# Exchanging the chunk parities of every second head in an RWKV-6 kernel, so that two bursts of quarter-array products stand side by side

## The chip, the cores and the metric

The kernel runs on one core of one Trainium2 chip. The metric is the device time of one execution in microseconds; the kernel before takes 603.1 us (median of 3 runs, 601.58 to 604.65). The profiled execution spans 601.8 us with a mean granted TensorE clock of 0.997.

## The reference, cut to what matters

The first half is a linear attention with a decaying state (RWKV-6, 4 batches, 8 heads, 768 steps, head size 48), the second a feed-forward block with an exact GELU:

```python
state = zeros((B, H, D, D))
for t in range(S):
    cur = einsum('bhd,bhe->bhde', u[None] * kt, vt)
    y[:, :, t] = einsum('bhd,bhde->bhe', rt, state + cur)
    state = wt[:, :, :, None] * state + einsum('bhd,bhe->bhde', kt, vt)
...
h = x @ w_in                    # 3072 x 384 by 384 x 2048
g = 0.5 * h * (1.0 + erf(h / sqrt(2)))
out = g @ w_out                 # by 2048 x 384
```

Everything is fp32.

## The kernel before, in words

**Segments.** The 4 x 768 steps are cut into 8 segments of T = 384 steps (`x` = 0 to 7); two follow each other in one batch, so every odd segment starts from the states of the segment before it. A segment has NC = 6 chunks of C = 64 steps. The 8 heads are taken as 4 pairs; in a pair, head g = 0 lies on partitions 0 to 63 and head g = 1 on partitions 64 to 127 (`half[g]`). Two pairs make a part b, so that index i (NI = 6) runs over the pairs of a part and the couples of chunks, and p is the parity of a chunk inside its couple.

**Attention of a segment**, `attention(x, unit)`, is a generator whose `yield`s cut it into slots:

1. Products of r and k within a chunk give the matrix of a chunk, built up by levels (`halves` for segments 0 and 1, `quarters` from segment 2 on). Each product is 64x64x64: contraction over `half[g]`, output on `half[p]` (`d[half[p], g, ...]`, L468 and L596). So four of them use the four quarters of the TensorE array at once. The results are copied into `a_sb` (`at`): parity p on `half[p]`, head g in the free dimension.
2. k is transposed, so that time lies on partitions: in segments 0 and 1 by whole TensorE transposes of 128x128 (L680), later by VectorE's transposes of 32x32 blocks, twelve small DMAs that move blocks (L542) and four copies on ScalarE (L690).
3. `kv` (L706): k transposed times v for each chunk, contraction over `half[p]`. VectorE's `chain_states` (L721, L726) makes from it the state at each chunk's start, one `scalar_tensor_tensor` for each chunk and pair of heads.
4. `y` = `inside` + the products with the states, summed in PSUM. `inside` (L747) multiplies v by the chunk's matrix: contraction over `half[p]`, output on `half[g ^ swap(b)]` of bank `p`. The products with the states (L791) contract over `half[g]` and write the same places. Where p differs from g, two products that add to one place come from different rows of the array. The `fences` between them are small VectorE copies that read the last element of each bank of `y` (L757, L759): they have to wait for `inside`, and the products with the states have to wait for them.
5. `y` goes to `xT`, the input of the feed-forward block: copies on ScalarE (L814, L817) and, for the fourth pair, six DMAs (L821).

PSUM holds `y` of one part as one tile of two banks (`pair`), a bank for each parity; only the first part of segment 0 (`split`) has two tiles of one bank. The tiles come from the same pool as `kv`, so `y` follows `kv` in its banks.

**The feed-forward block**, `mlp(x)`, runs on 128x128 weights: products h (L925, L1051), GELU on ScalarE, products with `w_out` (L1065, L1197), with sums of quarters (L917 to L921, L893) that save one product in eight. Results leave PSUM by ScalarE or VectorE (such as L1119, L1162, L1188).

**Order.** The scheduler is manual: each engine runs its instructions in the order of the program. That order is written out in `PLAN`: for each segment x a string whose letters take the next slot of a stream: "." `mlp(x - 1)`, "s" the attention of x, "f" the first slots of the attention of x + 1, "l" loads, "w" masks and sums of weights, "c" conversion of weights, "x" the sums of xT. Segment 0 isn't in `PLAN`; it runs before, with filler products (`keep_warm`) and the loads beside it.

In a slot for `y`, the lines that the change touches are these:

```python
inside()
fences()
yield
for i in range(NI):
    for p in range(2):
        for b in range(np_):
```

Of the kernel before, what the change touches and what calls it, by code (L numbers as in the profile page):

```python
# [10 lines left out]
F32 = mybir.dt.float32  # L11
# [9 lines left out]
C = 64  # L21
# [15 lines left out]
HALFWAY = 2  # L37
PLAN = {
    1: (
        "ccsc.cs...c.c.csccc.cs.sccc.l.csccccssc.cccs.c..cccs.sc.ccslcsc.scsclc.c.scssl.clc.wcsc.cc"  # L40
        "wsc.l.cs.cclcc.cc.wlwlcc.c.cwcs...wwfs..w...wfwl...s.w..f..wfw...wffffffffw"
    ),
    2: (
        ".......s.l.wsslw.swssss.s.s.sss.lssls.ssssssw..s.swl..w..ww.s.w.s.sslls.ll.slf.wfs..f.xxx."
        ".xx"
    ),
    3: (
        "ss.l....ss.ss...ls.sl.....s..s....sss.s..ss.ssss.ssl...ssls..ssss..ss...s.s..ls..sl..sslls"
        "f.s..fsf.fl.f.xx..xfxx"
    ),  # L50
    4: (
        "...s.s..ss...sl.s..s..l.ssl.ss.ssss.s.s.ss...sss..sssls.s.sls...s.s.l...slsls...sl.sf.fs.f"
        "xxx.lx...x"
    ),
    5: (
        "s.sl....s.s...slss...s.s.l...s....ssls.sls..s.ssssl.ss...ss.s.ss.sss..s.s.....s.ssls.s.l.l"
        "sf.s.ffs.ff..xx..xfxxl"
    ),
    6: (
        ".s..slss.......s.s.s...sll.ssls.sssssl..s.ss...sss..sssss....ssl..ss....slsss...lsl.sf...f"  # L60
        "xxl.xf..xx"
    ),
    7: (
        "s.s.s.s....s..ss.s...s...s.....ss.ss.s.ss.sss.ss...sss..ss.sssss.......s.s..sss.s..s.s...x"
        "xx..xx"
    ),
}

# [6 lines left out]
def kernel(  # L75
# [215 lines left out]
    def make_fine():  # L291
        nc.vector.tensor_tensor(out=fine_mask, in0=s_qs[FINE], in1=t_block, op=ALU.is_equal)
        nc.vector.tensor_tensor(out=later, in0=t_all, in1=s_qs[1], op=ALU.is_ge)
        nc.vector.tensor_tensor(out=fine_mask, in0=fine_mask, in1=later, op=ALU.bitwise_and)

        nc.gpsimd.memset(places, 0.0)
        for z in range(4):
            o = slice(z * 32, (z + 1) * 32)
            v = places[o]
            v = bass.AP(tensor=v.tensor, offset=v.offset, ap=[v.ap[0], [128 + 1, FINE], [FINE, 32]])  # L300
            nc.gpsimd.tensor_copy(out=v, in_=ident[o, o].unsqueeze(1).to_broadcast([32, FINE, 32]))

    def make_quarter_masks():
        make_fine()
# [64 lines left out]
    def attention(x, unit):  # L369
# [91 lines left out]
        def products(bs, right, width):  # L461
            d = pair("d")
            n = 0
            for b in bs:
                for i in range(NI):
                    for g in range(2):
                        for p in range(2):
                            nc.tensor.matmul(d[half[p], g, n * width:(n + 1) * width],  # L468
                                             lhsT=kc[half[g], b, i, p], rhs=right(half[g], b, i, p),
                                             start=True, stop=True)  # L470
                    n += 1
            return d[:, :, 0:n * width]
# [62 lines left out]
        kt_q = k.rearrange("p (g n d) -> p g n d", g=2, d=G)  # L535
        moves = [(src, dst) for dst in range(4) for src in range(4) if src != dst]

        def block_of_kt(dst, src):
            return kt_q[dst * 32:(dst + 1) * 32, src // 2, :, src % 2 * 32:src % 2 * 32 + 32]

        def move_block(dma, src, dst):
            dma.dma_start(out=block_of_kt(dst, src), in_=kb[src * 32:(src + 1) * 32, dst])  # L542

        def blocks_of_k():
            k32 = k.rearrange("p (n a j) -> p n a j", a=4, j=32)
# [5 lines left out]
        def quarters():  # L551
# [28 lines left out]
            for h in QUARTERS:  # L580
                m, r4, t4, s0, s1, s2 = views(h)

                def burst(first, behind):

                    d = pair("d")
                    if behind == n_b and h == FINE:
                        for a in range(FINE):
                            for g in range(2):
                                nc.tensor.matmul(fine_of(d, g)[:, a * n_b:], lhsT=places[half[g], a],  # L589
                                                 rhs=fine_sb[half[g], 0:FINE - a, a],  # L590
                                                 start=(a == 0), stop=True, skip_group_check=True)
                    for n in range(first, behind):
                        i = n - first
                        for g in range(2):
                            for p in range(2):
                                nc.tensor.matmul(d[half[p], g, i * 3 * C // 2:(i + 1) * 3 * C // 2],  # L596
                                                 lhsT=kc[half[g], n // NI, n % NI, p],
                                                 rhs=rx[half[g], 2 * n + p], start=True, stop=True)
                    return d
# [74 lines left out]
        if x < 2:  # L674
            kts = []
            for b in range(np_):
                kt_ps = pair("kt_ps")
                for i in range(NI):
                    o = (i % N3) * 128
                    nc.tensor.transpose(kt_ps[:, i // N3, o:o + 128], k[:, (b * NI + i) * 128:(b * NI + i + 1) * 128], ident)  # L680
                kt = kx[:, parts[b] * Q * T:(parts[b] + 1) * Q * T].rearrange("p (i g d) -> p i g d", g=2, d=G)
                nc.scalar.copy(out=kt.rearrange("p (b i) g d -> p b (i g d)", b=2), in_=kt_ps[:, :, 0:N3 * 128])
                kts.append(kt)

            def k_t(b, i, p, g):
                return kts[b][half[p], i, g, :]
        else:

            for z in range(4):
                nc.scalar.copy(out=block_of_kt(z, z), in_=kb[z * 32:(z + 1) * 32, z])  # L690

            def k_t(b, i, p, g):
                return kt_q[half[p], g, b * NI + i]
        yield

        def vs(b, i, g):
# [4 lines left out]
        for b in range(np_):  # L701
            kv_ps = pair("kv_ps")
            for i in range(NI):
                for p in range(2):
                    for g in range(2):
                        nc.tensor.matmul(kv_ps[half[g], p, i * D:(i + 1) * D], lhsT=k_t(b, i, p, g),  # L706
                                         rhs=vs(b, i, g)[half[p], 0:D], start=True, stop=True)
            kvs.append(kv_ps[:, :, 0:NI * D].rearrange("p c (q i e) -> p q i c e", q=Q, e=D))
        yield

# [22 lines left out]
        split = x == 0 and parts[0] == 0  # L733
        ys = []

        def inside():

            for b in range(np_):
                if split:
                    y = [ps.tile([128, BANK], F32, name="y_ps", tag="mm", bufs=2) for _ in range(2)]  # L740
                else:
                    y_ps = pair("y_ps")
                    y = [y_ps[:, c] for c in range(2)]
                for i in range(NI):
                    for p in range(2):
                        for g in range(2):
                            nc.tensor.matmul(y[p][half[g ^ swap(b)], i * C:(i + 1) * C], lhsT=vs(b, i, g)[half[p]],  # L747
                                             rhs=at[half[p], g, b * NI + i, :], start=(i == 0), stop=True, skip_group_check=True)
                ys.append((y, None if split else y_ps))

        def fences():

            for y, y_ps in ys:
                fence = wk.tile([128, 2], F32, name="fence")
                if split:
                    for c in range(2):
                        nc.vector.tensor_copy(out=fence[:, c:c + 1], in_=y[c][:, NI * C - 1:NI * C])  # L757
                else:
                    nc.vector.tensor_copy(out=fence, in_=y_ps[:, :, NI * C - 1])  # L759

        if x == 0:

            inside()
            yield
            for z in last_r:
                z()
            yield
            chain_states(range(NC - 1 + int(first)))
            fences()
            yield  # L770
        else:
            for c in range(0, NC, 2):
# [1 line left out]
                if x > 1 and c + 2 < NC:  # L774
                    yield
            yield
            inside()
            fences()
            yield

        for i in range(NI):
            for p in range(2):
                for b in range(np_):
                    q, c3 = divmod(i, N3)
                    for g in range(2):
                        c = 2 * c3 + (p + g) % 2
                        src, c0 = (st, c - 1) if c else (before, NC - 1)
                        if src is None:
                            continue
                        o = ((parts[b] * Q + q) * NC + c0) * D  # L790
                        nc.tensor.matmul(ys[b][0][c % 2][half[g ^ swap(b)], i * C:(i + 1) * C],  # L791
                                         lhsT=src[half[g], o:o + G], rhs=rc[half[g], b, i, c % 2],
                                         start=False, stop=True, skip_group_check=True)
        if split:
            for c, copy in enumerate((nc.scalar.copy, nc.vector.tensor_copy)):
                for z in range(2):
# [544 lines left out]
```

## Time and profile before

| engine | busy us | share of the span | instructions |
|---|---|---|---|
| TensorE, matmuls | 587.2 | 98% | 7442 |
| TensorE, weight loads | 514.3 | 85% | 7442 |
| VectorE | 459.9 | 76% | 878 |
| ScalarE | 261.3 | 43% | 604 |
| GpSimd | 8.4 | 1% | 24 |

| group | instructions | busy us | mean ns |
|---|---|---|---|
| `inside`, L747, matmul 64x64x64 | 768 | 13.8 | 222 |
| with the states, L791, matmul 64x64x64 | 704 | 14.4 | 225 |
| `kv`, L706, matmul | 768 | 14.6 | 220 and 227 |
| transposes of k, L680 | 24 | 3.1 | 274 |
| `fences`, L759 and L757, VectorE copy | 15 and 2 | 2.2 and 0.3 | 161 and 154 |
| states, L721, VectorE | 160 | 29.0 | 258 |

One fp32 product of the code is two matmul instructions in the trace (a transpose is one). The busy time of a group is the time in which at least one of its instructions runs; quarter-array products overlap four at a time, so 96 of them, 218 ns each, last only about 1.5 us.

By time, the segments' `y` bursts end near 43, 120, 185, 258, 322, 396, 459 and 533 us; from there to 601.8 us only the last feed-forward block remains. The first 44 us are segment 0, which is short of work for TensorE; after it, TensorE is busy nearly without a break.

### The profile page before, as it was taken

Reading aid. Unit: us, or ns where it says so; the run is one execution under the profiler, and the core shown is the slowest. Engines: PE = TensorE matmul, PEld = TensorE weight load, DVE = VectorE, ACT = ScalarE, POOL = GpSimd, SP = SyncE. Lnnn points to the kernel's source line nnn. Section 1 sums busy time; section 2 is a strip of 40 time slices with the busy share of each in tenths; the row PEclk is TensorE's granted clock in tenths of the full one; section 3 lists DMA queues with packets and bytes.
Section 4 is the critical chain, followed back from the end, with each engine's and each line's share of the span. In section 5 each row is a group of like instructions: output and inputs, shape, how many; then the busy total and the mean of one; then the engine's idle time right before and its main releaser. Section 6 shows DMA issues by size and latency. Waiting matters only on the chain.

```text
span 601.8 us, 17215 instructions
## 1 busy us (share of the span) xinstructions
PE 587.2 (98%) x7442; PEld 514.3 (85%) x7442; DVE 459.9 (76%) x878; ACT 261.3 (43%) x604; POOL 8.4 (1%) x24
## 2 busy tenths in 40 slices
PE   8879999999999999999999999999999999999997
PEld 4566666656699999999999999899999999989997
DVE  8979999998878977798857968798857979631211
ACT  2346656033433545245742554235652456225510
POOL 3100000000000000000000000000000000000000
PEclk9989999999999999999999999999999999999999
DMA  5739564120053101440052210413033100300000
GB/s 199 221 115 365 178 211 125 67 76 19 3 128 116 37 21 17 122 123 19 2 120 83 64 53 5 117 47 113 2 60 94 43 1 1 68 28 6 0 14 26
DMA packets 50571, 46.79 MB, mean 78 GB/s; under 512 B 31680, under 2 KB 35904, under 8 KB 50496
## 3 DMA queue, kind: packets, MB, share of 16 engines
q1 hardware_dynamic: 50400, 45.62, 25.0%
q8 instruction: 58, 0.95, 0.7%
q14 instruction: 17, 0.14, 0.1%
q10 hardware_dynamic: 96, 0.07, 0.1%
HBM read 36.24 MB, written 4.72 MB: 68 GB/s over the span
## 4 chain that ended last, share of the span: by engine, by line
PE 91%; DVE 2%; SPq 2%; issue 2%; DMA 1%; ACT 0%; DVEq 0%; ACTq 0%
PE o_ps L1065 27%; PE h_ps L925 16%; PE u_ps L925 13%; PE h_ps L1051 11%; PE o_ps L1197 5%; PE d L596 5%; PE d L468 3%; PE y_ps L791 2%; PE kv_ps L706 2%; PE y_ps L747 2%; PE u_ps L1065 2%; PE warm L240 2%; SPq L542 1%; SPq L821 1%; PE d L589 1%
## 5 line engine op out<-in xcount | busy, mean ns | idle before, releaser
L925 PE MATMUL h_ps<-xT,w_in_sb 128*128 128x192 f32 x480 | 96.3, 331 | 1.4 <-DVE o_sb L1162 0.8
L925 PEld LDWEIGHTS h_ps<-xT,w_in_sb 128*128 128x128 f32 x480 | 79.6, 190 | 5.3 <-DVE o_sb L1162 1.5
L1051 PE MATMUL h_ps<-xT,w_in_sb 128*128 128x384 f32 x192 | 64.5, 491 | 0.0
L1051 PEld LDWEIGHTS h_ps<-xT,w_in_sb 128*128 128x128 f32 x192 | 35.7, 190 | 23.6
L612 ACT COPY a_sb<-d 32x320 f32<-32x320 f32 (+5 forms) x108 | 39.2, 363 | 3.5 <-PE d L596 1.7
L1065 PE MATMUL o_ps<-w_out_sb,g 128*128 128x192 f32 x224 | 40.0, 327 | 0.0
L1065 PEld LDWEIGHTS o_ps<-w_out_sb,g 128*128 128x128 f32 x224 | 36.8, 190 | 0.6
L925 PE MATMUL u_ps<-s,w_in_sb 128*128 128x192 f32 x192 | 35.1, 326 | 0.0
L1197 PE MATMUL o_ps<-w_out_sb,g 128*128 128x384 f32 x96 | 32.9, 493 | 0.0
L925 PEld LDWEIGHTS u_ps<-s,w_in_sb 128*128 128x128 f32 x192 | 31.9, 190 | 0.0
L1054 ACT ACTIVATE g<-h_ps 128x384 f32<-128x384 f32 (+1 forms) x32 | 14.0, 436 | 40.3 <-PE h_ps L1051 40.3
L817 ACT COPY ysb<-y_ps 128x384 f32<-128x384 f32 x8 | 3.8, 480 | 60.9 <-PE y_ps L791 48.5
L1125 DVE TENSOR_TENSOR u<-o_ps,p 128x192 f32<-128x192 f32 x7 | 2.5, 358 | 36.0 <-PE o_ps L1065 36.0
L596 PE MATMUL d<-kx,rkw 64*64 64x96 f32 x1152 | 29.9, 247 | 0.0
L596 PEld LDWEIGHTS d<-kx,rkw 64*64 64x64 f32 x1152 | 24.9, 133 | 5.7 <-issue 3.2
L721 DVE SCALAR_TENSOR_TENSOR st<-st,tot_sb,kv_ps 128x48 f32<-128x48 f32 x160 | 29.0, 258 | 0.6 <-PE kv_ps L706 0.4
L979 DVE TENSOR_TENSOR g<-g,o_sb 128x384 f32<-128x384 f32 x24 | 13.2, 549 | 21.2 <-ACT o_sb L961 21.2
L1065 PE MATMUL o_ps<-w_out_sb,f 128*128 128x192 f32 x160 | 29.1, 331 | 0.0
L1065 PE MATMUL o_ps<-w_out_sb,e 128*128 128x192 f32 x160 | 28.5, 329 | 0.0
L1065 PE MATMUL o_ps<-t,g 128*128 128x192 f32 x160 | 28.4, 330 | 0.0
L468 PEld LDWEIGHTS d<-rkw 64*64 64x64 f32 x1152 | 18.7, 134 | 10.9 <-issue 3.9
L1065 PE MATMUL o_ps<-t,s 128*128 128x192 f32 x160 | 27.9, 327 | 0.0
(164 smaller groups left out, 1213.2 us busy)
## 6 DMA issues: line engine op xcount, KB each, us to landing
rkw<-in_rkw_dram SPq DMA_DIRECT2D x54, 256.0 KB, 3.5
raw<-in_w_out_dram SPq DMA_DIRECT2D x8, 768.0 KB, 4.5
v_in<-in_v_dram SPq DMA_DIRECT2D x8, 584.0 KB, 4.1
raw<-in_w_in_dram SPq DMA_DIRECT2D x5, 768.0 KB, 7.8
out_dram<-o_sb SPq DMA_DIRECT2D x20, 192.0 KB, 2.1
rkw<-kx SPq DMA_DIRECT2D x72, 48.0 KB, 2.1
raw<-in_w_in_dram SPq DMA_DIRECT2D x9, 256.0 KB, 3.4
rkw<-in_rkw_dram SPq DMA_DIRECT2D x8, 288.0 KB, 3.5
```

The source lines that it names most:

```text
L240: nc.tensor.matmul(t, lhsT=zeros[:, 0:128], rhs=zeros, start=True, stop=True)
L468: nc.tensor.matmul(d[half[p], g, n * width:(n + 1) * width], lhsT=kc[half[g], b, i, p], rhs=right(half[g], b, i, p), start=True, stop=True)
L596: nc.tensor.matmul(d[half[p], g, i * 3 * C // 2:(i + 1) * 3 * C // 2], lhsT=kc[half[g], n // NI, n % NI, p], rhs=rx[half[g], 2 * n + p], s ...
L612: nc.scalar.copy(out=at[z, :, first:behind, (a + 1) * h:], in_=d[z, :, :, o:o + (3 - a) * h])
L706: nc.tensor.matmul(kv_ps[half[g], p, i * D:(i + 1) * D], lhsT=k_t(b, i, p, g), rhs=vs(b, i, g)[half[p], 0:D], start=True, stop=True)
L721: nc.vector.scalar_tensor_tensor(out=stq[:, q, c], in0=stq[:, q, c - 1] if c else b4[:, q, NC - 1], scalar=totq[:, q, c:c + 1], in1=kvs[q ...
L925: nc.tensor.matmul(o, lhsT=lhsT, rhs=rhs, start=start, stop=True, skip_group_check=True)
L979: nc.vector.tensor_add(g_of(q, 0, 1), g_of(q, 0, 1), z)
L1051: nc.tensor.matmul(h_ps, lhsT=w_in_sb[:, f // FI, j, f % FI * 128:(f % FI + 1) * 128], rhs=xT[:, j, :], start=(j == 0), stop=(j == NJ - 1))
L1054: nc.scalar.activation(out=gs[group][:, f % FG, 0:t], in_=h_ps[:, 0:t], func=AF.Gelu)
L1065: nc.tensor.matmul(o, lhsT=lhs(j), rhs=rhs(j), start=start and j == 0, stop=(j == HF - 1), skip_group_check=True)
L1197: nc.tensor.matmul(o, lhsT=block(i, f // HF, f % HF), rhs=w_out_sb[:, f, :], start=(f == 0), stop=(f == NF - 1))
```

## The change

It exchanges, for head g = 1 of every pair, the two parities: the chunk of parity p now lies on `half[p ^ g]`. The matrices (`d`, `a_sb`), v (laid out so on the host), k transposed and the identity blocks in `places` follow. Then `inside` for the even chunks contracts over the same rows as the products with the states for the even chunks, and only the odd chunks come from other rows. The order becomes: `inside(1)`, the fence, `inside(0)`, the states for even chunks, the states for odd chunks. It is for having nothing of the other work between `inside` and the products with the states, so that both make one burst, with the fence's time covered by the even chunks. The fence reads only the odd chunks' bank, and moves from VectorE to ScalarE.

Two things follow. In segments 0 and 1 k is no longer transposed by whole transposes but by 64x64 products with the identity, four to a couple of chunks, since each quarter has to land elsewhere. And the slots of `y` are fewer by one from segment 2 on, so the whole `PLAN` is another one; slots of all streams stand in another order, the bursts of L596 and `kv` too.

```diff
-                            nc.tensor.matmul(d[half[p], g, n * width:(n + 1) * width],
+                            nc.tensor.matmul(d[half[p ^ g], g, n * width:(n + 1) * width],
...
-            v = bass.AP(tensor=v.tensor, offset=v.offset, ap=[v.ap[0], [128 + 1, FINE], [FINE, 32]])
-            nc.gpsimd.tensor_copy(out=v, in_=ident[o, o].unsqueeze(1).to_broadcast([32, FINE, 32]))
+            for part in range(2):
+                to = bass.AP(tensor=v.tensor, offset=v.offset + part * C, ap=[v.ap[0], [128 + 1, FINE], [FINE, 16]])
+                a = o.start + 16 * (part ^ z // 2)
+                nc.gpsimd.tensor_copy(out=to, in_=ident[o, a:a + 16].unsqueeze(1).to_broadcast([32, FINE, 16]))
...
-                    o = (i % N3) * 128
-                    nc.tensor.transpose(kt_ps[:, i // N3, o:o + 128], k[:, (b * NI + i) * 128:(b * NI + i + 1) * 128], ident)
+                    for p in range(2):
+                        for g in range(2):
+                            nc.tensor.matmul(kt_ps[half[p ^ g], g, i * G:(i + 1) * G], lhsT=kc[half[g], b, i, p],
+                                                rhs=ident[half[g], half[g]], start=True, stop=True)
...
+        def inside(c):
+            for i in range(NI):
+                for b in range(np_):
+                    for g in range(2):
+                        nc.tensor.matmul(ys[b][0][c][half[g ^ swap(b)], i * C:(i + 1) * C], lhsT=vs(b, i, g)[half[c ^ g]],
+                                         rhs=at[half[c ^ g], g, b * NI + i, :], start=(i == 0), stop=True, skip_group_check=True)
+
+        def before_chunks(par):
+            for i in range(NI):
+                for b in range(np_):
...
+                        nc.tensor.matmul(ys[b][0][par][half[g ^ swap(b)], i * C:(i + 1) * C],
+                                         lhsT=src[half[g], o:o + G], rhs=rc[half[g], b, i, par],
+                                         start=False, stop=True, skip_group_check=True)
 
         def fences():
 
-            for y, y_ps in ys:
-                fence = wk.tile([128, 2], F32, name="fence")
-                if split:
-                    for c in range(2):
-                        nc.vector.tensor_copy(out=fence[:, c:c + 1], in_=y[c][:, NI * C - 1:NI * C])
-                else:
-                    nc.vector.tensor_copy(out=fence, in_=y_ps[:, :, NI * C - 1])
+            for y, _ in ys:
+                fence = wk.tile([128, 1], F32, name="fence")
+                nc.scalar.copy(out=fence, in_=y[1][:, NI * C - 1:NI * C])
...
             yield
-            inside()
+            places_of_y()
+            inside(1)
             fences()
-            yield
-
-        for i in range(NI):
-            for p in range(2):
-                for b in range(np_):
...
+            inside(0)
+            if x == 1:
+                yield
+        before_chunks(0)
+        before_chunks(1)
...
+    a = a.copy()
+    a[:, :, 1] = a[:, :, 1, :, :, ::-1]
```

Of `PLAN`, the end of segment 3 shows the kind of change (before, then after):

```diff
-        "f.s..fsf.fl.f.xx..xfxx"
+        ".f.f.f.fsl.f.xx..xffffxx"
```

## The prediction

> **What bounds the kernel now.** I read the page's shares first, then the chain of waits, then the groups of the lines that the diff touches, then the order of weight loads in time around the two bursts.
>
> ```profile
> PE 587.2 (98%) x7442; PEld 514.3 (85%) x7442; DVE 459.9 (76%) x878; ACT 261.3 (43%) x604; POOL 8.4 (1%) x24
> PE 91%; DVE 2%; SPq 2%; issue 2%; DMA 1%; ACT 0%; DVEq 0%; ACTq 0%
> ```
>
> TensorE is busy 98% of the span and holds 91% of the chain. So only three things can move the time: TensorE work itself, its changes between the 128x128 products and the 64x64 quarter-array bursts, and the few moments in which it waits. The waits are listed by the waits view, TensorE alone:
>
> ```profile
> PE kv_ps L706 <- issue: 2.6, 1, 2.6
> PE warm L240 <- ACT zeros L232: 2.3, 1, 2.3
> PE kv_ps L706 <- DMA rkw<-kx: 1.6, 2, 1.1
> ...
> PE h_ps L925 <- DVE o_sb L1162: 0.8, 2, 0.4
> ...
> PE h_ps L925 <- DVE o_sb L1188: 0.6, 1, 0.6
> ```
>
> The fence is not among the large ones: outside the first segment its 15 VectorE copies hold nobody up, because output products stand between `inside` and the products with the states. The timeline of weight loads (start, length, engine, line, idle before) shows what the split costs instead:
>
> ```profile
> 317.81 1.49 PEld L747 LDWEIGHTS y_ps<-a_sb,v_in 64*64 64x64 f32 x96 [0.23 <-issue]
> 319.37 1.27 PEld L1065 LDWEIGHTS o_ps<-w_out_sb,e 128*128 128x128 f32 x8
> 320.87 1.26 PEld L791 LDWEIGHTS y_ps<-rkw,st 64*64 64x64 f32 x80 [0.23 <-issue]
> 322.19 1.27 PEld L1065 LDWEIGHTS o_ps<-w_out_sb,e 128*128 128x128 f32 x8
> ```
>
> Eight 128x192 products take 1.30 us in the chain (8 at 0.1625), but 1.50 us pass from 319.37 to 320.87: entering a burst costs 0.20. The 96 loads of L747 start 14.3 ns apart, 1.37 us in all, but 1.56 us pass to 319.37: leaving costs 0.19. **A round trip is 0.39 us** (in segment 1, with 384-wide products, 5.35 us for sixteen that need 5.24, so 0.30).
>
> [...]
>
> **The change, part by part.**
>
> *Bursts that merge.* In segments 1 to 7 `inside` and the products with the states stand side by side. Six round trips of 0.39 and one of 0.30: **-2.6 us**. The new plan also joins the two half bursts of L596 at 418 us: -0.4.
>
> *The fence.* It is meant to lie behind `inside(0)` and `before_chunks(0)`, the fenced products being only `before_chunks(1)`. But the built program says otherwise: in segments 1 to 7 the first product of `inside(0)` for each pair of heads waits for ScalarE's fence copy of its tile (L777 of the changed file). Both parities lie in one PSUM tile there; only where each parity has a tile of its own (first segment, second unit) does the wait stand at `before_chunks(1)`. TensorE issues in order, so everything behind it stands still: the rest of the burst, then the output products. The length of this stop can be read off the one place where the fence was exposed before:
>
> ```profile
> 39.92 1.11 PE L747 MATMUL y_ps<-a_sb,v_in 64*64 64x64 f32 x44
> ...
> 41.06 0.23 DVE L757 COPY fence<-y_ps 128x1 f32<-128x1 f32 x2 [0.85 <-PE y_ps L747]
> ...
> 41.34 1.38 PE L791 MATMUL y_ps<-rkw,st 64*64 64x64 f32 x40 [0.31 <-DVE fence L757]
> ```
>
> The last matmul of L747 starts at 40.81 (218 ns long), two VectorE copies take 0.23, the next load starts at 41.34: 0.53 us where 0.014 is usual. [...] I take 0.57, seven times: **+4.0 us**. Low end 0.35 (only the first copy counts), high end 0.75 (ScalarE still busy; it waits idle at `ysb` L817 in before, 48.5 us over six times, so this is unlikely).
>
> *k transposed by quarter products in segments 0 and 1.* 12 whole transposes become 96 matmul instructions. In segment 1, 1.60 us (L680, 95.35 to 96.95) become 1.56 as for any burst of 96, plus 0.1 for entering: +0.1. The ScalarE copy keeps its 768 columns.
>
> *Nothing:* 17 VectorE fences go (2.7 us), off the path since VectorE only waited there; GpSimd's `places` go from 4 copies to 8 halves on an engine with 1% (ready at 17 us, read in segment 2); v is laid out before the launch.
>
> *The plan moves the bursts.* I compared the order on TensorE; one 128x192 product of the code is two instructions, 0.325 us.
> - `kv` waits for the moved blocks of k in segments 3 and 5. Their 96 loads take 2.31 and 2.98 us instead of 1.36, so 0.95 and 1.62 are lost. In the new order 44 output products instead of 40 lie ahead in both: 1.3 us more. **-2.2 us**.
> - `kv` to `y`: in segment 7 eight products (2.6 us, 2.95 with leaving and entering) instead of twelve; VectorE's chain of states ends 3.35 us after `kv` (524.00 + 3.24 against 523.93), and `y` takes over the bank that it reads. **+0.4 us**. Twelve elsewhere is enough, as before.
> - `y` to the next h: T is the end of `y`. In segment 4 (before) the DMA of xT lands at T+5.9, four subtractions (L893) 0.39 apart, then L1162 frees h's second bank at T+7.7, while TensorE is there at T+7.3 (20 products, leaving, 0.65 of h): the 0.4 above. In the new order segment 3 has 16 products instead of 20: TensorE at T+6.05, bank free at T+6.8 (landing T+5.7, two subtractions, then L1199 of the changed file, which frees it): +0.8. Segment 5 has 24 (T+8.65), but L1199 stands behind three subtractions, L1192, two L1195 (again lines of the changed file) and two more subtractions: T+9.2, +0.55. Segments 2, 4, 6 and 7 come out as before within 0.2. **+1.4 us**.
>
> *Segment 0.* With one pair of heads, `inside(c)` uses two quarters at a time; the trace has 17 ns a load for four (0.80 for 48) and 31 for two (1.25 for 40): +0.7 for each unit. The first unit's fence queues on ScalarE behind L345 and L346 (33.03 to 34.85), about +0.5. Against this, 0.3 of exposed fence goes, and TensorE stands idle for 2.6 us from 34.73 in the middle of a burst, with nothing to wait for; one 16 KB packet of the instruction queue starts at 34.9, so I read it as instructions that come late. Part of the extra work falls into that hole. I take 0, from -1.1 to +1.2.
>
> Sum: -2.6 - 0.4 + 4.0 + 0.1 - 2.2 + 0.4 + 1.4 + 0 = +0.7, so **603.8 us**: the round trips saved and the waits mended are paid back by the new stop inside each burst.
>
> **Rivals.** *Faster:* the fence costs 0.35 each (-1.5), the h waits stay as they were (-1.4), segment 7 doesn't wait (-0.4), and the first segment gains 1.1: 603.1 + 0.7 - 4.4 = 599.4. For it: DMA landings vary, and VectorE is a little freer. Against it: the two fence copies are in series. *Slower:* the fence costs 0.75 (+1.3), only half of the `kv` waits goes (+1.1), the first segment loses 1.2: 607.4. For it: the stop is in every segment, the gain from later `kv` only in two, and 192 matmuls in a row need instructions faster than any stretch of before. Against it: ScalarE is idle there.
>
> **How the numbers follow.** 0.5 for 603.8; 0.25 for each rival. Half a per cent is 3.0 us, so the three chances are the three cases. The range reaches 0.4 to 0.6 past the centre of each rival, so that under 0.2 is left out, and takes in both ends of the fence's cost: 599.0 to 608.0.
>
> **What would show it.** Right: in the weight loads of segments 1 to 7 one burst of 192 (or 176), with a stop of 0.5 to 0.6 us after the first 48, put down to ScalarE's fence; some 14 fence copies on ScalarE of about 0.16 us; `kv` bursts in segments 3 and 5 of 1.4 and 1.7 us. Wrong: no stop there (599 to 600), a stop of 0.8 or more (607), or waits of over 1 us at h or `kv` that I have not listed.

## The result, and the profile after

| | us, median | runs | ratio to the kernel before (95% interval) |
|---|---|---|---|
| before | 603.3 (601.58 to 604.65) | 4 | |
| changed | 610.1 (609.47 to 611.51) | 4 | 1.0117 (1.0085 to 1.0150) |

The changed kernel is slower by about 7 us; the prediction was 603.8, with a range to 608.0. The profiled executions, 608.7 and 601.8 us, differ by 6.9. The page of the changed kernel, its shares and its chain:

```profile
PE 587.7 (97%) x7592; PEld 517.0 (85%) x7610; DVE 458.4 (75%) x861; ACT 262.8 (43%) x620; POOL 8.5 (1%) x28
...
PE 90%; DVE 5%; issue 2%; ACT 1%; SPq 0%; DMA 0%; ACTq 0%; DVEq 0%
```

TensorE is still what bounds the kernel, and it is busy for as long as before: 587.7 against 587.2 us. So what was added is time in which it stands still. The waits view of the changed kernel, TensorE alone (total, times, longest):

```profile
PE y_ps L769 <- issue: 2.6, 4, 1.0
...
PE y_ps L756 <- ACT fence L777: 1.9, 8, 0.3
...
PE o_ps L1076 <- issue: 1.6, 2, 1.0
PE y_ps L769 <- ACT fence L777: 1.0, 1, 1.0
```

The fence is there, as forecast. The `kv` waits of before on the DMA of blocks (1.6 us, segments 3 and 5) are gone. New are six waits for "issue", that is for nothing the profile names, in the products with the states (L769) or in the output products right behind them (L1076). In what follows the fence's wait is a stop, and a wait of this new kind a stall. The timeline of weight loads in segment 3 shows both kinds in one burst:

```profile
259.65 0.79 PEld L756 LDWEIGHTS y_ps<-a_sb,v_in 64*64 64x64 f32 x48 [0.22 <-issue]
260.83 0.78 PEld L756 LDWEIGHTS y_ps<-a_sb,v_in 64*64 64x64 f32 x46 [0.38 <-ACT fence L777]
...
261.58 1.49 PEld L769 LDWEIGHTS y_ps<-rkw,st 64*64 64x64 f32 x94
263.13 0.46 PEld L1076 LDWEIGHTS o_ps<-t,s 128*128 128x128 f32 x3
264.89 1.27 PEld L1076 LDWEIGHTS o_ps<-t,s 128*128 128x128 f32 x8 [1.30 <-issue]
```

Between the 48 loads of `inside(1)` and those of `inside(0)` lies the fence's stop (0.52 us from load to load, where 0.014 is usual). The burst then runs to its end, three output products follow, and TensorE stands still for 1.3 us with everything ready. Taken from load to load, less the usual distance, these stalls are 0.45, 0.95, 1.33, 0.72, 1.20 and 1.00 us in segments 1, 2, 3, 5, 6 and 7, and none in segment 4: **5.65 us**.

**What the stalls have in common.** I numbered TensorE's instructions in the order of the program, the loads and matmuls of each product singly (an fp32 product is a load, a matmul, a load, a matmul: four; a whole transpose or a filler product is two) and the semaphore instructions too: 15,369 in all, for 7610 loads, as many matmuls (a few of their records are missing in the page) and 149 others. The page's DMA part counts this for the instruction queue:

```profile
q8 instruction: 60, 0.98, 0.7%
```

60 packets of 16 KB for 15,369 instructions are 256 instructions to a packet. Each of the six stalls stands at an instruction whose number is 194 or 195 modulo 256 (called a packet end below), and so do the three that break into bursts of segment 0 (0.2, 0.5 and 2.1 us); each ends 1.27 to 1.50 us after a packet of that queue has landed. So TensorE waits there for its own instructions, by this reading; the next section tests it. How soon TensorE comes from one packet end to the next depends on what it runs: in output products, at 81 ns an instruction, 256 last 21 us; in a quarter-array burst, at 7.15 ns, 1.83 us. In the stalls of segments 1 to 3 it took 2.8 to 3.8 us from one packet end (the places 194) to the moment at which the instructions behind the next one ran: 0.4 to 0.9 us until the packet starts, 1.0 to 1.5 for the packet, 1.35 to 1.41 behind it. In segment 4, which has no stall, the packet starts 0.5 us before TensorE reaches the packet end. A burst of 192 loads is 384 instructions, enough to hold two packet ends; one of 96, as before, is 192.

The end of segment 0, ScalarE's timeline of the changed kernel:

```profile
42.39 0.48 ACT L828 COPY ysb<-y_ps 128x384 f32<-128x384 f32 x1 [4.43 <-PE y_ps L769]
42.89 1.87 ACTq L832 DMA_DIRECT2D xT<-ysb  x3
44.81 0.16 ACT L777 COPY fence<-y_ps 128x1 f32<-128x1 f32 x1 [1.95 <-PE y_ps L769]
```

The second unit's fence could not start before ScalarE had issued three DMAs of the first unit's `ysb` (1.87 us); TensorE waited 0.98 us for it, the last wait line above. Segment 0's last product with the states stands at 45.66 us, against 42.45 before: **+3.2**.

### The profile page after: what moved, and what is told of

It reads as the page before. It is cut to its first block, busy times and chain, and to the rows that moved or that the text cites. A ratio compares the mean times of both kernels' runs of the same rounds, so it can differ in the third digit from the quotient of the medians.

```text
span 608.7 us, 17535 instructions
## 1 busy us (share of the span) xinstructions
PE 587.7 (97%) x7592; PEld 517.0 (85%) x7610; DVE 458.4 (75%) x861; ACT 262.8 (43%) x620; POOL 8.5 (1%) x28
## 4 chain that ended last, share of the span: by engine, by line
PE 90%; DVE 5%; issue 2%; ACT 1%; SPq 0%; DMA 0%; ACTq 0%; DVEq 0%
PE o_ps L1076 28%; PE h_ps L936 15%; PE u_ps L936 12%; PE h_ps L1062 10%; PE o_ps L1208 5%; PE d L601 4%; PE d L470 3%; PE y_ps L756 2%; PE kv_ps L714 2%; PE y_ps L769 2%; PE u_ps L1076 2%; PE warm L240 1%; PE d L594 1%; DVE tot_sb L429 1%; PE kt_ps L686 1%
## 5 line engine op out<-in xcount | busy, mean ns | idle before, releaser
L1062 PE MATMUL h_ps<-xT,w_in_sb 128*128 128x384 f32 x192 | 64.5, 491 | 0.1
L1062 PEld LDWEIGHTS h_ps<-xT,w_in_sb 128*128 128x128 f32 x192 | 35.8, 190 | 23.6
L1076 PE MATMUL o_ps<-w_out_sb,g 128*128 128x192 f32 x224 | 40.0, 328 | 0.0
L1076 PEld LDWEIGHTS o_ps<-w_out_sb,g 128*128 128x128 f32 x224 | 36.8, 190 | 0.6
L729 DVE SCALAR_TENSOR_TENSOR st<-st,tot_sb,kv_ps 128x48 f32<-128x48 f32 x160 | 29.0, 257 | 1.9 <-PE kv_ps L714 1.8
L626 DVE COPY_PREDICATED a_sb<-quarter,d 128x480 f32<-128x480 uint8 (+5 forms) x54 | 23.2, 438 | 9.4 <-PE d L601 8.2
L1076 PE MATMUL o_ps<-t,s 128*128 128x192 f32 x160 | 28.2, 329 | 1.0 <-issue 1.0
L1076 PE MATMUL o_ps<-w_out_sb,f 128*128 128x192 f32 x160 | 28.3, 328 | 0.6 <-issue 0.6
L1076 PE MATMUL o_ps<-t,g 128*128 128x192 f32 x160 | 28.5, 330 | 0.0
L1076 PE MATMUL o_ps<-w_out_sb,e 128*128 128x192 f32 x160 | 28.4, 329 | 0.0
L470 PEld LDWEIGHTS d<-rkw 64*64 64x64 f32 x1152 | 18.8, 136 | 10.7 <-DVE rkw L517 4.8
```

What stands on the lines that cost most here:

```text
L470: nc.tensor.matmul(d[half[p ^ g], g, n * width:(n + 1) * width], lhsT=kc[half[g], b, i, p], rhs=right(half[g], b, i, p), start=True, stop= ...
L626: nc.vector.copy_predicated(out=an[:, :, :, :, (a + 1) * h:], mask=mask.to_broadcast(data.shape), data=data)
L729: nc.vector.scalar_tensor_tensor(out=stq[:, q, c], in0=stq[:, q, c - 1] if c else b4[:, q, NC - 1], scalar=totq[:, q, c:c + 1], in1=kvs[q ...
L1062: nc.tensor.matmul(h_ps, lhsT=w_in_sb[:, f // FI, j, f % FI * 128:(f % FI + 1) * 128], rhs=xT[:, j, :], start=(j == 0), stop=(j == NJ - 1))
L1076: nc.tensor.matmul(o, lhsT=lhs(j), rhs=rhs(j), start=start and j == 0, stop=(j == HF - 1), skip_group_check=True)
```

## The experiments

Two theories go in. "Instruction supply": the unnamed stalls are packets that come too late, so they depend on where the packet ends lie in a burst. The rival: they belong to the burst itself (banks, the fence, the number of products), or the fence alone explains the loss.

### Moving the packet ends

```diff
-    keep_warm(6, True)
+    t = pair("warm")
+    for n in range(31):            # 53 in the second kernel
+        g, p = n // 2 % 2, n % 2
+        nc.tensor.matmul(t[half[p ^ g], g, 0:C], lhsT=ident[half[g], half[g]], rhs=ident[half[g], half[g]], start=True, stop=True)
```

> The changed kernel (610.1) with the six filler products at the end of segment 0 replaced by 31 quarter products with the identity, which are 112 more instructions on TensorE and at most 0.5 us more work; nothing else differs. Theory 'instruction supply': TensorE's instructions come in packets of 256, and every unexplained stall of the changed kernel stands where one packet ends (instruction 194 or 195, modulo 256); two such ends inside one fast burst are too close. With 112 more instructions the first packet end lies at instruction 170 (segment 1), 216 (2), 23 (3), 181 (4), 22 (5), 148 (6) and 243 (7) of the y bursts. So the stalls of segments 1, 2, 6 and 7 (0.5, 0.95, 1.2, 1.0 us) go or nearly go, those of 3 and 5 stay at 0.5 to 1.0 but move from just behind the burst to inside it, and segment 4 still has none: -2.5 to -3.5 us, so about 607. Rival 'local': the stalls belong to what a burst does (fence, banks, number of products), then they stay in the same segments and the time is 610.1 to 610.6.

> As the run with 112 more instructions, but with 53 quarter products, which are 200 more instructions and about 1.0 us more work in segment 0. Instruction supply: packet ends at instruction 82 (segment 1), 128 (2), 191 (3), 93 (4), 190 (5), 60 (6) and 155 (7) of the y bursts, so now segments 1, 2, 4 and 6 stall (0.5 to 1.2 us each) and 3, 5 and 7 don't: the other set than with 112, with segment 4, which never stalled before, among them. About -2 us for the stalls, +1.0 for the added work: 609. Local: stalls in the same segments as in the changed kernel, and 611.

Measured: 611.95 us, ratio 1.0148 (1.0124 to 1.0172), and 616.84, ratio 1.0218 (1.0191 to 1.0245). The times went the wrong way, but the stalls went with the packet ends, with three misses in 14 (segments 3 and 7 with 112 more, segment 2 with 200 more):

| first packet end in the burst (instruction), stall in us | seg. 1 | 2 | 3 | 4 | 5 | 6 | 7 |
|---|---|---|---|---|---|---|---|
| changed | 26: 0.45 | 72: 0.95 | 135: 1.33 | 37: 0 | 134: 0.72 | 4: 1.20 | 99: 1.00 |
| 112 more | 170: 0 | 216: 0 | 23: 0 | 181: 0 | 22: 0.40 | 148: 0 | 243: 0.64 |
| 200 more | 82: 0.85 | 128: 0 | 191: 0 | 93: 0.64 | 190: 0 | 60: 0.88 | 155: 0 |

Segment 3 of the run with 200 more, with the same lines as the fence above, has its stop but no stall (1.49 us of loads, then output products at once), while segment 4, which never stalled in the changed kernel, now does:

```profile
268.07 1.49 PEld L769 LDWEIGHTS y_ps<-rkw,st 64*64 64x64 f32 x94
269.63 1.44 PEld L1076 LDWEIGHTS o_ps<-t,s 128*128 128x128 f32 x9
...
331.47 1.25 PEld L769 LDWEIGHTS y_ps<-rkw,st 64*64 64x64 f32 x76
333.24 0.19 PEld L769 LDWEIGHTS y_ps<-rkw,st 64*64 64x64 f32 x2 [0.52 <-issue]
```

Over the seven kernels of this study with merged bursts and the fence on ScalarE, segments 1 to 7, none of the 15 bursts whose first packet end lies at 148 to 216 stalled, and 28 of the other 34 did. The starts of the packets tell most of the rest: in all 28 the packet began 0.2 to 2.5 us after TensorE had passed the packet end before the stall, and in five of the six that escaped it had begun 0.5 to 2.9 us ahead of that. (In the sixth, segment 2 with 200 more, the next packet end lies behind the burst.) The local rival falls.

Why the times rose shows in the same view, where the added products stand (L1257, run with 200 more):

```profile
44.67 1.75 PEld L1257 LDWEIGHTS warm<-ident 64*64 64x64 f32 x105
46.29 0.89 PEld L470 LDWEIGHTS d<-rkw 64*64 64x64 f32 x49
51.50 1.37 PEld L470 LDWEIGHTS d<-rkw 64*64 64x64 f32 x47 [4.32 <-issue]
```

I had added to one burst what I took from others: behind 106 added loads the burst of `d` (L470) stood still, at an instruction of number 194 modulo 256 again, for 4.3 us (4.1 with 112 more); the packet began only 3.7 to 4.0 us behind the packet end there. Behind the stall four (112 more) or seven (200 more) loads of L1062 stood 0.64 us apart instead of 0.32; the clock that TensorE was granted is 0.50 in that stretch of both traces (3.4 and 6.8 us). My expectation priced those products by their work alone.

The second run also answers a step of the prediction: without the stalls behind `y` of segments 3 and 5, TensorE reaches h earlier and waits there. Beyond the usual distance of two loads it is 0.83 us in segment 5 (the last line) and 0.37 in segment 3, too short for these lines (the first is segments 2 and 6).

```profile
PE h_ps L936 <- DVE o_sb L1173: 0.9, 2, 0.6
PE h_ps L936 <- DVE o_sb L1199: 0.5, 1, 0.5
```

### The fence off the path

```diff
-                else:
+                elif x == 0:
                     y_ps = pair("y_ps")
-                    ys.append(([y_ps[:, c] for c in range(2)], y_ps))
+                    ys.append(([y_ps[:, c] for c in range(2)], None))
+            if x > 0:
+                odd, even = pair("y_ps"), pair("y_ps")
+                ys.extend(([even[:, b], odd[:, b]], odd) for b in range(np_))
...
+                nc.scalar.copy(out=fence, in_=ys[0][1][:, :, NI * C - 1])
```

> The changed kernel with y of segments 1 to 7 laid out by parity: one tile of two banks holds the odd chunks of both parts, the other the even chunks. So the products of the even chunks no longer wait for the fence, which stands in front of the odd chunks' products with the states only; one fence copy instead of two; and the copies from y are twice as many with half the columns (ScalarE about +1 us a segment, off the path unless h waits). Theory 'fence alone': the stop of 0.53 us goes in seven segments and nothing takes its place: -3.7, so 606.4. Instruction supply: in segments 1, 2 and 6 the packet end lies ahead of the fence (instructions 26, 72 and 4), so the burst still ends when the next packet is there and the stall inside grows by what the stop loses; in segment 4 (37) a stall of up to 0.5 appears; only segments 3, 5 and 7 gain 0.53 each: -1.0 to -1.6, so 608.8.

Measured: 607.35 us, ratio 1.0065 (1.0043 to 1.0087), about 2.8 less than the changed kernel. Segment 3:

```profile
257.82 1.49 PEld L759 LDWEIGHTS y_ps<-a_sb,v_in 64*64 64x64 f32 x96 [0.23 <-issue]
259.21 1.50 PEld L772 LDWEIGHTS y_ps<-rkw,st 64*64 64x64 f32 x96
260.77 0.46 PEld L1085 LDWEIGHTS o_ps<-t,s 128*128 128x128 f32 x3
262.13 1.92 PEld L1085 LDWEIGHTS o_ps<-t,s 128*128 128x128 f32 x12 [0.90 <-issue]
```

The stop is gone, the stall at the same instruction stays. In all, stalls of 0.87, 0.93, 0.76, 1.16 and 1.63 us in segments 2, 3, 5, 6 and 7 sum to 5.35, so they took back less of the stop than I expected (only in segment 7 did the stall grow, by 0.63, more than the stop of 0.42). `inside` and the products with the states lost 3.1 us between them; `kv` took 0.7 back, by a wait in segment 6. In this kernel the fence, with the layout of `y` that goes with it, is worth about 3 us, and the stalls stay almost what they were. No run here leaves the fence out, so what it guards against is not shown.

### Segment 0 as before

```diff
-                            nc.tensor.matmul(d[half[p ^ g], g, n * width:(n + 1) * width],
+                            nc.tensor.matmul(d[half[p ^ g if x else p], g, n * width:(n + 1) * width],
...
+                if x == 0:
...
+                        nc.tensor.transpose(kt_ps[:, i // N3, o:o + 128], k[:, (b * NI + i) * 128:(b * NI + i + 1) * 128], ident)
...
+    a[0, :, 1, 0] = a[0, :, 1, 0, :, ::-1]
```

(For x = 0, `inside`, the fences and the products with the states are those of before as well. The first kernel also has 39 of the added products above.)

> The changed kernel with segment 0 as in the kernel before (k transposed whole, inside by whole chunks, fences on VectorE, v of segment 0 laid out as before), and 39 quarter products in place of the six filler products at its end, so that from segment 1 on every instruction has the same place in its packet as in the changed kernel. Theory: segment 0 is worth the 3.2 us by which its end (45.66 against 42.45 us) came later, and the other segments keep their stalls: 606.9 plus up to 0.6 for the added products. Rival: what segment 0 loses is hidden later, since VectorE and the loads of segment 1 set the pace there: 609.5 to 610.1.

> The changed kernel with segment 0 as in the kernel before, and no added products this time, so that all later instructions come 144 places earlier, which is the same place in a packet of 256 as with 112 more. Theory: -3.2 for segment 0, and the stalls of the y bursts as with 112 more (0.4 in segment 5, 0.65 in segment 7, none elsewhere) instead of 5.2: 602.8, no slower than the kernel before, with every fence stop still in it. Rival 'the count of instructions doesn't matter': 606.9. Rival 'segment 0 is hidden later': 606 to 610.

Neither kernel has the places in the packets that its expectation gives. There a whole transpose counts as four instructions; in the trace it is two, and segment 0 has 12. So all that follows stands 24 places earlier than in the changed kernel (with the 39 products) or than in the run with 112 more (without them). The first packet ends of the `y` bursts of segments 1 to 7 are 50, 96, 158, 60, 157, 28 and 123 with them, 194, 240, 46, 205, 45, 172 and 11 without.

Measured: 610.02 us, ratio 1.0108 (1.0085 to 1.0132), with the 39 products; **605.02**, ratio 1.0027 (1.0012 to 1.0042), without. The two kernels differ in these products (78 loads, 1.1 us, in place of 0.9 us of filler) and in the place of everything behind them in its packet; together that is worth 5.0 us. With them, the burst of `d` behind them stalls 1.65 and 1.17 us,

```profile
43.27 1.02 PEld L470 LDWEIGHTS d<-rkw 64*64 64x64 f32 x63 [1.53 <-issue]
...
50.34 0.78 PEld L470 LDWEIGHTS d<-kx,rkw 64*64 64x64 f32 x45 [1.05 <-issue]
```

and the `y` bursts 5.8 us in all, in segments 1, 2, 4, 6 and 7; without, only segments 3, 5 and 7 stall (1.06, 0.93 and 1.44), 3.4 us. Both sets are those that the packet ends name, except that segment 2 of the second escapes.

The median of the first kernel is that of the changed one (610.10), as the rival said. Its profile shows why this doesn't speak against the theory: segment 0 ends 5.7 us earlier than in the changed kernel (39.91), behind the two stalls of `d` 3.2 of that are left at `y` of segment 1, and 1.9 at the end (606.8 against 608.7).

How much of it is segment 0? Its end varies between kernels that have the same code there. In some traces the granted clock falls to 0.50 for 3.4 us in this segment; the kernel before (37.0 to 40.4 us) and the changed one (38.4 to 41.8) are among them. With such a stretch, segment 0 as before ends at 42.4 us (two traces) and the changed one at 45.6 to 46.2 (four). Without it, they end at 39.8 to 42.2 (six) and at 44.7 (one; the kernel below with its fences on VectorE is left out). So the changed segment 0 costs some 3 to 4 us.

### Both together

The two edits above in one kernel.

> Segment 0 as in the kernel before and y of segments 1 to 7 laid out by parity, so that the fence stops nothing. Theory: the two add up. 602.8 for segment 0 and the places in the packets, and 3.4 less for seven stops: 599.4. Rival: without the stops the instruction supply takes the time back in more segments, 601.5 to 603.

Measured: 603.12 us, ratio 0.9994 (0.9975 to 1.0012): the time of the kernel before, not the 599.4 expected. Without stops the four remaining stalls (segments 2, 3, 5, 7) are 1.33 to 1.59 us each, 5.7 in all. That is the rival's account: in segments 3, 5 and 7 the burst that no longer stops for the fence passes from one packet end to the next in 1.83 to 1.87 us instead of 2.32 to 2.38. How much of that a stall takes back depends on the packet too: in the kernel with the fence off the path alone, the instructions were there 2.8 to 3.4 us behind a packet end in segments 2, 3 and 6, instead of 3.3 to 3.8, and the stalls hardly grew.

### y cut again, and the order alone

```diff
             inside(0)
-            if x == 1:
-                yield
+            yield
         before_chunks(0)
```

(with one more "s" behind the next "." of each string of `PLAN`; and, second, the kernel before with that `PLAN`)

> The changed kernel with the slot of y cut again in two, between inside and the products with the states, one slot of output products between them; parities, fence on ScalarE and segment 0 stay as changed. Instruction supply: no burst of y has more than 192 instructions, so the stalls of 0.5 to 1.2 us in and behind them go (5.2 us in all); the fence's stop of 0.53 stays in each; seven round trips between 64x64 and 128x128 come back (+2.6): about -2.6, 607.5. Rival 'merging is right and the stalls have another cause': the stalls stay and the round trips are added, 612.7.

> The kernel before (y in two slots, fences on VectorE, no exchange of parities) with the order of slots of the changed kernel, one slot of y added behind the next output slot. It takes the order alone. Theory: kv of segments 3 and 5 no longer waits for blocks of k (-2.5), the half bursts of L596 are joined once (-0.4), the waits of h are 1.0 shorter: 599.2. Rival 'the new order is part of what makes the changed kernel slower': 603 or more.

Measured: 616.40 us, ratio 1.0196 (1.0167 to 1.0224), and 614.67, ratio 1.0171 (1.0142 to 1.0200). They miss what was expected by 9 and 15 us. No `y` burst of the cut kernel has a stall for instructions of over 0.2 us, as expected. But the cut put the end of `y` one slot (four products, 1.3 us) later, with h where it was. The waits views, the cut kernel and then the order alone:

```profile
PE h_ps L935 <- DVE o_sb L1172: 3.3, 3, 1.4
...
PE h_ps L935 <- DVE o_sb L1198: 1.8, 3, 0.8
```

```profile
PE h_ps L925 <- DVE o_sb L1162: 4.4, 3, 1.7
PE y_ps L791 <- DVE fence L759: 4.1, 3, 3.1
```

h begins only after the copies of `y` to `xT`, their DMAs and a few VectorE operations; one slot less in between costs over 5 us in six segments. So merging `y` seems to have bought more than round trips: with one slot fewer the new order could move `kv` later and leave y where it was. And in this order a fence on VectorE stands behind work of the next segment. In the second kernel two `y` bursts of only 96 loads stall for instructions, by 0.5 and 0.3 us (segments 1 and 6): with one slot between them, `inside` and the products with the states still run 256 instructions in 3.3 to 3.4 us. Neither run isolates what I meant it to.

### The fence on VectorE

```diff
-                nc.scalar.copy(out=fence, in_=y[1][:, NI * C - 1:NI * C])
+                nc.vector.tensor_copy(out=fence, in_=y[1][:, NI * C - 1:NI * C])
```

> The changed kernel with its fences on VectorE instead of ScalarE, nothing else. It takes back one part of the change. Theory: in segments 1 to 7 the stop stays, since the products of the even chunks wait for the fence whichever engine runs it: 0.53 us each if VectorE is free, up to 1.0 where it is in the middle of an operation (segments 1 to 7: 0 to +3). In segment 0 the second unit's odd chunks waited 0.98 us for a fence that ScalarE could not start before it had issued three DMAs; on VectorE the fence stands behind a copy of the states only, so up to 1.0 us is won there. 609 to 613. Rival 'the fence's engine is the cause': 603 to 606.

Measured: 625.10 us, ratio 1.0382 (1.0350 to 1.0414). The wait on the fence grows from 1.9 us to

```profile
PE y_ps L756 <- DVE fence L777: 13.6, 8, 4.6
```

and VectorE's timeline shows what stands ahead of it in segment 3:

```profile
262.20 3.04 DVE L409 SCALAR_TENSOR_TENSOR kx<-rkw,u_sb,rkw 128x384 f32<-128x384 f32 x4
...
265.34 1.76 DVE L396 TRANSPOSE_TENSOR_REDUCE rkw<-kx 128x48 f32<-128x1536 f32 x1
...
270.68 0.22 DVE L777 COPY fence<-y_ps 128x1 f32<-128x1 f32 x2
```

The first slots of the next segment ("f") lie ahead of `y` in the new order. ScalarE is right for this fence, by 15 us; I had looked at whether VectorE was free, not at what was queued on it. In segment 0 it brings nothing: the second unit then waits for VectorE's states (L729; 1.6 us in three waits).

### y cut behind the fence

```diff
             inside(1)
             fences()
+            yield
             inside(0)
-            if x == 1:
-                yield
```

(with one more "s" ahead of the "." before the last "s", and segment 0 as before)

> The kernel with segment 0 as before and the rest as changed (605.0), with y cut behind the fence: the odd chunks' inside (48 loads) one slot of output products earlier, then four such products, then the rest of y in its place, so the end of y moves no later with respect to h. It hides the fence and cuts the instructions of a burst without touching the distance from y to h, which the cut behind inside did touch (there six waits at h of 0.4 to 1.5 us appeared). Theory: -3.7 for seven stops, -2.6 for the remaining stalls (0.8, 0.7 and 1.2 in segments 3, 5 and 7), +2.6 for seven round trips, up to +2.4 where inside now stands 8 products behind kv and waits for the chain of states: 601.5 to 603.7, with waits at h of under 1 us in all. Rival 'cutting itself costs what the cut kernel lost': 611 or more.

Measured: 604.74 us, ratio 1.0050 (1.0037 to 1.0063): not faster than the uncut one (1.0027). Stops and stalls in `y` are gone (5.7 us in the kernel without the cut), and the waits at h stay at 0.5, but seven round trips are back, and `inside`, one slot closer to `kv`, waits for the states:

```profile
PE y_ps L763 <- DVE st L736: 3.6, 4, 1.6
```

### kv later, in the kernel before

```diff
-        ...ls..sl..sslls        # PLAN[3]
+        ...ls...sl.sslls
-        ...s.ssls.s.l.l         # PLAN[5]
+        ...s.s.slss.l.l
```

> The kernel before with kv of segments 3 and 5 one slot of output products (four products, 1.3 us) later, as in the changed kernel, and nothing else moved: the end of y stays where it was. It takes alone the part of the new order that the prediction priced at -2.2. Theory: the two kv bursts lose 0.95 and 1.62 us in before; 1.3 us later they lose 0 and 0.3. In segment 3 only 8 instead of 12 products then lie between kv and inside, which waits for VectorE's chain of states by up to 0.5; in segment 5 there are 12. So -1.8 in all: 601.3. Rival 'the lost time comes back as a wait for the states or for h': 602.5 to 603.5.

That first try (612.26 us, ratio 1.0179, 1.0146 to 1.0211) put the load of the next segment ahead of `kv`, which waited 4.1 and 3.4 us for it and read its data, so its time says nothing about the question. The second keeps `kv` ahead of that load:

> The kernel before with kv of segments 3 and 5 four products (1.3 us) later, now still ahead of the load of the next segment. (In the earlier try of this edit that load stood ahead of kv, so that kv read the next segment's data and waited for its transfer; its time doesn't answer the question.) Nothing else moves. Theory: kv loses 0.95 and 1.62 us in the kernel before, 0 and 0.3 here; in segment 3 inside then stands 8 products behind kv instead of 12 and waits up to 0.5 for the states: -1.8 in all, a ratio of 0.997 to the kernel before. Rival 'the lost time comes back as a wait for the states or for h': a ratio of 0.999 to 1.001.

Measured: **600.06 us, ratio 0.9957 (0.9943 to 0.9971)**, faster than both kernels. `kv` of segment 3 is a plain burst again (2.31 us before from first to last load, now 1.36), and that of segment 5 takes 1.70 instead of 2.98; `inside` of segment 3 waits 0.3. Segment 3 in the kernel before, and with `kv` later:

```profile
245.40 0.45 PEld L706 LDWEIGHTS kv_ps<-v_in,rkw 64*64 64x64 f32 x6 [0.23 <-issue]
246.37 1.47 PEld L706 LDWEIGHTS kv_ps<-v_in,rkw 64*64 64x64 f32 x90 [0.53 <-issue]
```

```profile
245.55 1.49 PEld L706 LDWEIGHTS kv_ps<-v_in,rkw 64*64 64x64 f32 x96 [0.23 <-issue]
247.09 1.27 PEld L1065 LDWEIGHTS o_ps<-t,g 128*128 128x128 f32 x8
```

## Why the prediction was wrong, step by step

| step | predicted us | found in the two traces |
|---|---|---|
| round trips saved, half bursts joined | -3.0 | -2.7 (46 entries into quarter-array products after segment 0 instead of 53) |
| stop of the fence, segments 1 to 7 | +4.0 | +3.4 (0.50 six times, 0.42) |
| `kv` of segments 3 and 5 | -2.2 | -2.6 |
| `y` behind `kv` in segment 7 | +0.4 | +0.35 |
| waits of h | +1.4 | -1.0 (0.4 us of TensorE idle instead of 1.4) |
| segment 0 | 0 | +3.2 |
| instruction supply in `y` | not in the sum | +5.65 |
| sum | +0.7 | +6.3; the spans differ by 6.9 |

- **The step that failed most** is the first one, in what it took for granted: that a merged burst runs at 14.3 ns a load all the way. The prediction names the objection ("192 matmuls in a row need instructions faster than any stretch of before") as an argument for the slower rival, and gives it no price. It is the largest term. The trace of before held what was needed: its unnamed stalls of 2.86 us at 34.5, of 0.6 at 90.3 and of 0.3 at 26.1 stand at instructions 1731, 3522 and 1218, all 194 or 195 modulo 256. I read the first as instructions that come late, and priced it for segment 0 only. The two moved runs show that the stalls go with the packet ends, with three misses in 14. Two kernels that differ in 39 small products and in the places, 610.0 and 605.0, show what it can be worth: 2.4 us in the `y` bursts and 2.8 in `d`.
- **Segment 0** was taken as 0 in a range to +1.2, on the reasoning that the added work falls into the hole in which TensorE stands idle. The hole was shorter by 0.8 and swallowed nothing, and the prediction looked only at the first unit's fence, not at the second's (1.0 us of TensorE idle). In the two traces the 3.2 us are +0.5 up to the first transpose (where kernels with the same code differ by up to 2 us), +0.9 in the transposes (half of it a stall for instructions), and +1.8 from `kv` to the end of `y`, with `inside` by two quarters, both fences and the shorter hole in it. These parts are read off the traces; the runs show only the whole, 3 to 4 us.
- **The waits of h.** The 0.8 and 0.55 foreseen in segments 3 and 5 did not come because the stalls behind `y` there (1.33 and 0.72 us) held TensorE back. In the run with 200 more instructions, where those two are free of stalls, the loads of h wait 0.37 and 0.83: the step was about right for an execution without stalls. The -1.0 is another thing, that the old waits of segments 4 and 7 (0.4 and 0.6) are gone, where the prediction had no change of over 0.2. They are gone in the run with 200 more as well, where segment 7 has no stall; the reason is open.
- **Right** were the reading that the fence stops the even chunks too, its place behind the first 48 loads and its size (0.57 was the author's estimate, near the 0.53 measured behind two VectorE copies; 0.50 came, with two ScalarE copies in 0.22 us, 160 ns each, 16 in all), the round trips, `kv`, and `y` behind it in segment 7 (the 3.35 us for the chain of states are 3.31 by the figures beside them, so 0.36 instead of 0.4). `kv` alone, put into the kernel before, gives -2.6 us.

What stays open: 0.6 us between sum and spans, and 0.6 more because the stall of before at 90.3 us, which the changed kernel doesn't have, is not in the table; and why a packet starts ahead of TensorE once and up to 2.5 us behind it another time.

## What to carry to other kernels

Before two fast bursts are merged, count their instructions and compare with the packets of the instruction queue: here 256 quarter-array instructions last 1.8 us, 2.8 to 3.8 us passed in three stalls from one packet end to the instructions behind the next, and of the 34 `y` bursts whose first packet end lay outside 148 to 216, 28 stalled, by 0.4 to 1.7 us, more than the round trip of 0.39 us that the merge saves. A cheap fence still needs a tile of its own (about 3 us here), and an engine on which nothing long is queued ahead of it (15 us). And when a change comes with a new order, try the order's moves one by one: the best of it, two `kv` slots moved by four products each, was worth more without the rest.

## What the runs showed of the hardware

In the seven kernels with merged bursts, the 28 stalls of their `y` end 1.22 to 1.57 us after a packet of the instruction queue has landed. Instructions added for no work at all (39 products in place of filler, 0.2 us more) changed a kernel of 605.0 us by 5.0 us: `d` behind them stalled for 1.65 and 1.17 us, and the `y` bursts for 5.8 us in all instead of 3.4. At the end of the stalls of 4.1 and 4.3 us in `d`, with 112 and 200 more instructions, the granted clock of TensorE was 0.50 for 3.4 and 6.8 us: loads for 384-column products stood 0.64 us apart there, twice the usual 0.32. In segment 0 it was 0.50 for 3.4 us as well: in the kernel before from 37.0 to 40.4 us, where a stall of 2.86 us in `kv` ends at 37.3, and in the changed one from 38.4 to 41.8, where a stall of 2.1 ends at 36.8.
